# Token mixing by Fourier transform and a gated feed-forward block: stage one contracts residues j and 47-j together, in 64-column tiles

## The chip, the core and the metric

The kernel runs on one core of a Trainium2 chip. A core has a matrix engine (PE, also TensorE), which multiplies a stationary operand (the weights, loaded by a weight-load instruction, "PEld") with a moving one and writes to an accumulator memory, PSUM; a vector engine (DVE), a scalar engine (ACT), a general engine (POOL, GpSimd), and a queue engine (SP) that issues most of the DMA transfers. Each engine takes its instructions in order; they wait for each other by semaphores. The metric is the device time of one execution, in microseconds (us).

## The reference, cut to what matters

```python
def _attn_ref(x):                      # x: 8 x 3008 x 256, float32
    X = np.fft.fft(x, axis=1)          # over the tokens
    X = np.fft.fft(X, axis=2)          # over the channels
    return X.real.astype(np.float32)

def _moe_ref(x, w_gate, w_val, w_out): # x: 24064 x 256, d_ff = 1536
    g = x @ w_gate
    gelu = 0.5 * g * (1.0 + erf(g / np.sqrt(2.0)))
    val = x @ w_val
    return (gelu * val @ w_out).astype(np.float32)
```

The second function takes the first one's output as 24064 tokens.

## The kernel before, in words

The transform over the channels is folded into the weights, so that what is left per batch is the transform over 3008 tokens, of which the real part and its mirror image are used, and the feed-forward block.

The token transform is done in two stages, with 3008 = 64 x 47: token 47 n + j, with n from 0 to 63 and residue j from 0 to 46. The names are `N1` = 64, `N2` = 47, `HJ` = 24 (half the residues), `KP` (the rows of stage two).

*Loading and folding.* `load_x` brings a third of a batch at a time (8 residues of each half) into one of three buffers `xin`. Partition 2n holds residue j, partition 2n+1 residue j+24, for j from 0 to 23. `fold_x` adds and subtracts channel c and channel 256-c (two products on POOL or, for the first batch, DVE) and writes `xf`, bf16, 24 residues x 2 halves (even, odd) x 128 channels; `singles` copies the two channels without a partner on POOL.

*Stage one.* `a_step(b, k)` multiplies two residue slots of `xf`: each is one product with 128 weight columns of `G` (128 partitions x 128 columns, in which the two residues that share the partitions have blocks of their own and the rest is zero) and 256 moving columns. So a product gives 64 frequencies for each of two residues. The two products fill one PSUM bank, and ACT (for three of them DVE) copies it as bf16 to `S1`. There are 12 steps in a batch. `z_write` sends parts of `S1` to HBM, `z_read` brings them back turned into `Ap`, with the 96 residue rows on partitions (two rows for each of 48 slots, `KP` = 96) and 32 frequencies x 256 channels along them. For the first batch `a_group(J)` does the same in six groups of sixteen products with 32 weight columns each, in turn on four column positions, and turns the result from `S1` to `Ap` by one DMA inside the chip.

*Stage two.* `b_steps(b, eo, q)` makes the products with `Ap` as weights (96 rows x 128 columns) and a table `TP` or `TQ` as the moving operand (47 columns): 66 a batch in two halves (`eo`) and four blocks (`q`). For the first batch 33 more with one weight column. Evacuated, they give `Y`. `n_turn` and `n_step` do the same for one single channel, in f32, with 48 weight columns.

*The feed-forward block.* A batch is 36 units (3 column chunks x 12 blocks of d_ff), some 2 us each. A unit has four or five products of 128x128 weights and 480 to 512 columns (`layer1`, weights `WE`, `WOP`, `WOM`), its activations on ACT, its products of gate and value on DVE and POOL, and six or eight products of the second layer with 256 columns (`second`, weights `h`), which belong to the chunk before.

*Order.* The order is written out by hand in the main loop (from line 955 on); each engine keeps the program's order. While batch b runs its units, batch b+1 is prepared between them: `a_step(b + 1, k)` at the end of units 0 to 11 (for batch 1 at units 4 to 15, `a_first`), its writes after steps 5, 7 and 11, its reads at units 8, 10 and 13; stage two at units 18 to 26 (odd half) and 27 to 34 (even half), as `fills`: two products at a time between two of `layer1`. x of batch b+2 is loaded at units 0, 14 and 19, and folded on POOL at the odd units from 5 on. All x, z and output transfers go through SP's one queue. `ps_d`, one PSUM bank, serves `a_step`, `b_steps` and `n_step` after the start.

```python
        def fill(most=2):
            for _ in range(most):
                if fills:
                    fills.pop(0)()
```

Of the kernel before, what the change touches and what calls it, by code (L numbers as in the profile page):

```python
# [9 lines left out]
FP32 = mybir.dt.float32  # L10
BF16 = mybir.dt.bfloat16
AF = mybir.ActivationFunctionType
ALU = mybir.AluOpType
# [24 lines left out]
def kernel(  # L38
# [28 lines left out]
    HJ = 24  # L67
    KP = 96
    NG = 32
# [45 lines left out]
    col_j = const_pool.tile([128, 1], FP32)  # L115
    prow = const_pool.tile([1, 641], BF16)
    cols = const_pool.tile([128, 5], FP32)
    col_w = const_pool.tile([128, 1], FP32)
# [6 lines left out]
    def S1_tile():  # L125
        return work.tile([128, HJ, C], BF16, tag="S1", bufs=1, name="S1")

# [63 lines left out]
    def ps_o():  # L191
        return psum.tile([128, 512], FP32, tag="o", bufs=1, name="ps_o")
# [4 lines left out]
    def z_tile():  # L197
        return dram.tile([HJ, 128, C], BF16, tag="z", bufs=2, name="z")


    def load_x(b, i):
        xt = xins[i]
        for o, n, nh in ([(0, 7, 2), (7, 1, 1)] if i == 2 else [(0, 8, 2)]):
            src = ap_replace(
                x, ap=[[N2 * C, N1], [HJ * C, nh], [1, n * C]],
                offset=x.offset + (b * T + 8 * i + o) * C)
            p_step = xt[:, :, :].ap[0][0]
            dst = ap_replace(
                xt[:, :, :], ap=[[p_step * 2 // nh, N1 * nh], [1, n * C]],
                offset=xt[:, :, :].offset + o * C)  # L210
            sync.dma_start(out=dst, in_=src)
# [22 lines left out]

    vec.memset(xins[2][:, 7, :], 0.0)
    for i in range(3):
# [10 lines left out]
    row = lambda i, pat, off=0: _sub(prow, pat, 128 * i + off, 0, 1)  # L247
    for k in range(2):
        iota(row(0, [[24, 4], [6, 2], [3, 2], [1, 3]], 12 * k), [[1, 4], [0, 2], [4, 2], [8, 3]], 24 * k, 0)
    for i, (base, sign) in enumerate(((0, 1), (0, 1), (1, -1))):  # L250
        iota(row(1 + i, [[12, 8], [6, 2], [1, 6]]), [[0, 8], [sign, 2], [0, 6]], base, 0)
    pool.memset(row(0, [[128, 4], [1, 32]], KP), 0.0)
    pool.memset(row(4, [[1, 129]]), 1.0)

    def cols_t():
        ps = ps_o()
        for i in range(5):
            pe.matmul(ps[:, i : i + 1], _sub(prow, [[1, 128]], 128 * i, 0, 1),
                      _sub(prow, [[1, 1]], 640, 0, 1), start=True, stop=True)
        vec.tensor_copy(cols, ps[:, :5])  # L260
        vec.tensor_scalar(col_j, cols[:, 0:1], 1.0 / N2, None, op0=ALU.mult)
        vec.tensor_scalar(col_w, cols[:, 4:5], -TWO_PI, None, op0=ALU.mult)
# [46 lines left out]

    whole(col_f, col_p, 0.5, -0.25)  # L310
    vec.tensor_scalar(col_a, col_p, 360.0, None, op0=ALU.mult)
    vec.scalar_tensor_tensor(col_a, col_f, -719.0, col_a, op0=ALU.mult, op1=ALU.add)
    vec.tensor_scalar(rowj, rowj, col_a, None, op0=ALU.add)
    vec.scalar_tensor_tensor(col_b, col_f, -2.0, col_p, op0=ALU.mult, op1=ALU.add)
    vec.tensor_scalar(col_h[1], col_b, -TWO_PI, None, op0=ALU.mult)
    vec.tensor_scalar(col_h[0], col_b, TWO_PI, -TWO_PI, op0=ALU.mult, op1=ALU.add)

# [168 lines left out]
    def a_step(b, k):  # L486

        if "S1" not in st[b]:
            st[b]["S1"] = S1_tile()
        S1 = st[b]["S1"]  # L490
        if b == 0:
            ps = (ps_g, ps_vh, ps_o if k % 8 < 4 else ps_d, ps_vh)[k % 4]()
        else:
            ps = ps_o() if b == 1 and k in (3, 5) else ps_d()
# [18 lines left out]
    def a_group(J):  # L513
        if "S1" not in st[0]:
            st[0]["S1"] = S1_tile()
        S1 = st[0]["S1"]
        if J % 4 < 2:
            ps, log = ps_v(), []
            both = ps
            banks = [(ps[:, h, :], log) for h in range(2)]  # L520
        else:
            banks = [(f(), []) for f in ((ps_g, ps_g) if J % 4 == 2 else (ps_o, ps_d))]
        for gq in range(4):
            for jl in range(4):
                jj = 4 * J + jl
                ps, log = banks[gq // 2]
                apart(log, gq // 2, pe.matmul(
                    _sub(ps, [[1, C]], gq % 2 * C, 32 * jl, 32),
                    _sub(G, [[32, 4], [4, 8]], (jj - 16 * (J > 3 and gq % 2 == 0)) * 128 + gq),
                    _sub(xf, [[1, C]], jj * C), start=True, stop=True))  # L530
        if J > 3:
            for o, n, scale in ((0, 2, 1.0), (2, 1, -1.0), (3, 1, 1.0)):
                ps, log = banks[o // 2]
                to, of = _sub(S1, [[1, n * C]], (4 * J + o) * C), _sub(ps, [[1, n * C]], o % 2 * C)
                apart(log, o // 2, vec.tensor_scalar(to, of, scale, None, op0=ALU.mult) if J == 4 and o else
                      act.activation(to, of, AF.Copy, scale=scale))
        if J < 2:
            act.activation(_sub(S1, [[1, 4 * C]], 4 * J * C), both, AF.Copy)
        for h in range(2 * (J in (2, 3))):
            dst = _sub(S1, [[1, 2 * C]], (4 * J + 2 * h) * C)  # L540
            act.activation(dst, banks[h][0], AF.Copy)
        p_step = Ap[:, :, :].ap[0][0]
        sync.dma_start(
            out=ap_replace(
                Ap[:, :, :], ap=[[6 * p_step, 16], [1, NG * C]],
                offset=Ap[:, :, :].offset + (J % 2 * 3 + J // 2) * p_step),
            in_=_sub(S1, [[1, 4 * C]], 4 * J * C))

    def z_read(b, third, h=None):
        z = st[b]["z"]  # L550
        src = ap_replace(
            z[0:1, 0, :], ap=[[NG * C, 16], [16 * NG * C, 2], [1, NG * C]][:: 1 if h is None else 2],
            offset=z[8 * third + 4 * (h or 0), 0:1, :].offset)
        p_step = Ap[:, :, :].ap[0][0]
        dst = ap_replace(
            Ap[:, :, :], ap=[[3 * p_step, 32] if h is None else [6 * p_step, 16], [1, NG * C]],
            offset=Ap[:, :, :].offset + (third + 3 * (h or 0)) * p_step)
        sync.dma_start(out=dst, in_=src)
# [374 lines left out]
    for f0, o, n, us, turn in (  # L933
# [6 lines left out]
    extra[7].append(gen_wn)  # L940
    a_first = {4: (0,), 5: (1,), 8: (2, 3), 9: (4,), 10: (5, 6)} | {
        11 + j: (7 + j,) for j in range(5)}
    reads_first = {12: (0,), 14: (1,), 16: (2, 0), 17: (2, 1)}

# [10 lines left out]
    for u in range(NU + 2):  # L955
# [82 lines left out]
        if u < NU:  # L1038
            if b == 0:
                for e in extra.get(i, ()):  # L1040
                    e()
                if i < 12:
                    fold_x(1, i // 4, pool, i % 4 * 2, 2)
            if i % 2 and b + 2 < B:
                j = i - 1
                if b:
                    f, fp = next((j - o, n) for n, o, z in ((0, 4, 18), (1, 18, 28), (2, 28, 36)) if j < z)
                else:
                    fp, f = divmod(j - 12, 8)
                if 0 <= f < 8 and fp >= 0:  # L1050
                    fold_x(b + 2, fp, pool, f, 2)
            if b + 1 < B:
                for k in (i,) if b else a_first.get(i, ()):
                    if k < 12:
                        a_step(b + 1, k)
                        if k in ((5, 7, 11) if b else (5, 7, 9, 11)):
                            j0 = {5: 0, 7: 12, 9: 16, 11: 16 if b else 20}[k]
                            z_write(b + 1, j0, 2 * k + 2 - j0)
                    if b and k in (8, 10, 13):
                        z_read(b + 1, (8, 10, 13).index(k))  # L1060
                if b == 0 and i in reads_first:
                    z_read(1, *reads_first[i])
        if 0 < u <= NU and u % 12 == 0:
# [41 lines left out]
```

## Time and profile before

| | us |
|---|---|
| median of three runs (616.19 to 616.27) | 616.2 |
| the profiled execution | 616.14 |
| its span, by the profile | 614.3 |
| the start, until the first product of unit 0 | 23.8 |
| stretch of 70 us in the middle: PE / DVE / ACT / POOL busy | 69.62 / 66.72 / 57.20 / 63.46 |

Some of the groups of PE by shape, in the profile's view of instruction groups (line, engine, operation, output<-inputs, weight rows x weight columns, operands; count; busy time and mean ns of one):

```profile
L25 PE MATMUL ps_d<-xf,G 128*128 128x256 bf16 x164 | 31.2, 272 | 0.0
L25 PE MATMUL ps_d<-TP,Ap 96*128 96x47 bf16 x217 | 22.4, 185 | 0.3
L25 PE MATMUL ps_d<-TQ,Ap 96*128 96x47 bf16 x225 | 21.7, 185 | 0.7
L25 PE MATMUL ps_v<-xf,G 128*32 128x256 bf16 x64 | 3.3, 370 | 3.9 <-POOL xf L25 3.9
L25 PE MATMUL ps_d<-NA,TF 96*48 96x31 f32 x28 | 2.5, 213 | 0.0
```

The mean of one is the time from its start to its modelled end. Products follow each other before the one ahead has ended, so what a product takes of PE is the distance from its start to the next one's, which the timeline shows; a group's line doesn't. A few per cent of the records are missing (164 of 168 here). Nearly every instruction has line 25, that of the helper which records the order; the tiles' names tell them apart.

### The profile page before, as it was taken

The page shows a single profiled execution, that of the slowest core. Times are in us where ns is not written, and L with a number is a line of the kernel's source. Part 1 is how long each engine was busy: PE and PEld are TensorE (multiplying, and loading weights), DVE is VectorE, ACT ScalarE, POOL GpSimd, SP SyncE. Part 2 cuts the span into 40 slices and gives each one's busy share as a digit, 9 for nine tenths or more (in the row PEclk, how much of TensorE's full clock was granted, in tenths as well). Part 3 has the DMA queues.
Part 4 walks back from the last instruction along what each step waited for, and adds up shares of the span by engine and source line. Part 5 has one row for each costly group of instructions (what it writes and reads, how often), then busy time and mean ns, then how long its engine had stood idle before and what let it go on. Part 6 is the DMA issues. An engine that isn't in the chain of part 4 may idle for free.

```text
span 614.3 us, 13104 instructions
## 1 busy us (share of the span) xinstructions
PE 597.6 (97%) x4581; PEld 399.8 (65%) x4638; DVE 567.2 (92%) x689; ACT 487.4 (79%) x1011; POOL 501.5 (82%) x525
## 2 busy tenths in 40 slices
PE   4999999999999999999999999999999999999997
PEld 2556666666676666666667666766667666666666
DVE  8788999999999999999999999999999999999992
ACT  8798789877898787977789778887789878776762
POOL 5599999989999899798998899898997755665552
PEclk9999999999999999999999999999999999999999
DMA  7989424772257612674246633476223712222123
GB/s 277 348 233 264 135 65 116 202 216 60 61 149 197 197 39 70 205 224 113 66 120 173 192 93 74 121 207 209 46 67 100 203 37 52 59 47 52 39 48 86
DMA packets 63459, 80.79 MB, mean 132 GB/s; under 512 B 8186, under 2 KB 56826, under 8 KB 60674
## 3 DMA queue, kind: packets, MB, share of 16 engines
q1 hardware_dynamic: 61682, 79.05, 45.5%
q0 software_dynamic: 1552, 0.79, 0.9%
q8 instruction: 36, 0.59, 0.4%
q14 instruction: 29, 0.24, 0.1%
q10 hardware_dynamic: 160, 0.13, 0.1%
HBM read 43.47 MB, written 35.68 MB: 129 GB/s over the span
## 4 chain that ended last, share of the span: by engine, by line
PE 91%; ACT 3%; DMA 2%; DVE 2%; SPq 1%; issue 1%; ACTq 0%; POOL 0%
PE ps_o L25 38%; PE ps_g L25 26%; PE ps_v L25 20%; PE ps_d L25 7%; DMA xin<-in_x_dram 1%; ACT glm L25 1%; ACT osb L25 1%; ACT S L25 1%; SPq L850 1%; DMA out_dram<-osb 1%; ACT glp L25 0%; DVE h L25 0%; SPq L855 0%; DVE red L25 0%; DVE ev L25 0%
## 5 line engine op out<-in xcount | busy, mean ns | idle before, releaser
L25 POOL TENSOR_TENSOR h<-glm,dv 128x1024 bf16<-128x1024 bf16 (+1 forms) x138 | 290.8, 2109 | 80.6 <-DVE dv L25 60.0
L25 PE MATMUL ps_o<-Wo_sb,h 128*128 128x256 bf16 x2124 | 284.2, 272 | 1.0
L25 PEld LDWEIGHTS <-h 128*128 128x128 bf16 x2208 | 211.0, 98 | 58.3 <-issue 0.9
L25 DVE SCALAR_TENSOR_TENSOR ev<-nq,WN,ps_v 128x512 f32<-128x512 bf16 (+1 forms) x276 | 202.2, 734 | 23.4 <-PE ps_v L25 13.4
L25 ACT ACTIVATE glp<-ps_g 128x512 bf16<-128x512 f32 (+1 forms) x288 | 169.8, 590 | 37.2 <-PE ps_v L25 18.6
L25 ACT ACTIVATE glm<-ps_g 128x512 bf16<-128x512 f32 (+1 forms) x241 | 142.2, 590 | 56.6 <-PE ps_g L25 44.0
L25 DVE TENSOR_TENSOR h<-glp,ps_v 128x1024 bf16<-128x1024 bf16 (+2 forms) x150 | 173.0, 1154 | 4.2 <-ACT glp L25 3.5
L25 DVE SCALAR_TENSOR_TENSOR dv<-ev,ps_v 128x1024 f32<-128x1024 f32 (+1 forms) x138 | 164.9, 1195 | 0.0
L25 POOL TENSOR_TENSOR xf<-xin 128x254 bf16<-128x254 f32 x168 | 118.1, 724 | 0.4 <-PE ps_g L25 0.4
L25 PE MATMUL ps_v<-Y,WOP 128*128 128x512 bf16 (+1 forms) x288 | 107.7, 374 | 0.1
L25 PE MATMUL ps_v<-Y,WE 128*128 128x512 bf16 (+1 forms) x286 | 107.3, 375 | 0.0
L25 PE MATMUL ps_g<-Y,WE 128*128 128x512 bf16 (+1 forms) x266 | 99.3, 373 | 0.0
L25 PE MATMUL ps_g<-Y,WOP 128*128 128x512 bf16 (+1 forms) x257 | 96.0, 373 | 0.8
L25 PE MATMUL ps_g<-Y,WOM 128*128 128x512 bf16 (+1 forms) x241 | 90.3, 375 | 0.2
L25 PEld LDWEIGHTS <-WOP 128*128 128x128 bf16 x576 | 55.5, 97 | 49.2 <-ACT WOP L25 0.6
L25 PEld LDWEIGHTS <-WE 128*128 128x128 bf16 x576 | 56.0, 97 | 27.8 <-issue 2.0
L25 ACT ACTIVATE osb<-ps_o 128x512 f32<-128x512 f32 x92 | 54.2, 589 | 13.4 <-PE ps_o L25 11.9
L25 POOL TENSOR_TENSOR go<-go,ge 128x480 f32<-128x480 f32 (+1 forms) x47 | 58.1, 1236 | 7.1 <-DVE go L25 7.1
L25 PEld LDWEIGHTS <-Ap 96*128 96x128 bf16 (+1 forms) x561 | 39.6, 96 | 31.7 <-issue 0.2
L25 ACT ACTIVATE S<-ps_d 128x512 bf16<-128x512 f32 x82 | 48.9, 596 | 0.2 <-PE ps_d L25 0.2
L25 PEld LDWEIGHTS <-G 128*128 128x128 bf16 (+1 forms) x289 | 22.0, 110 | 26.5 <-issue 4.7
L25 DVE SCALAR_TENSOR_TENSOR go<-nq,WN,ps_g 128x480 f32<-128x480 bf16 (+1 forms) x47 | 34.3, 730 | 2.6 <-ACT glp L25 1.9
(134 smaller groups left out, 371.8 us busy)
## 6 DMA issues: line engine op xcount, KB each, us to landing
out_dram<-osb SPq DMA_DIRECT2D x358, 64.0 KB
xin<-in_x_dram SPq DMA_DIRECT2D x16, 1024.0 KB
Ap<-z SPq DMA_DIRECT2D x20, 512.0 KB
xin<-in_x_dram SPq DMA_DIRECT2D x8, 896.0 KB
z<-S SPq DMA_DIRECT2D x7, 768.0 KB
z<-S SPq DMA_DIRECT2D x6, 512.0 KB
nq<-nrow SPq DMA_DIRECT2D x8, 376.2 KB
z<-S SPq DMA_DIRECT2D x9, 256.0 KB
```

Source lines behind the costliest of these rows:

```text
L25: return lambda *a, **k: self._tc.keep_in_program_order(call(*a, **k))
L850: queues[q % 2].dma_start(out=rows_ap(rows[0][0], 32, rows[1][0] - rows[0][0], 2), in_=_sub(t, [[C, 2], [1, C]], 0, 32 * q, 32))
```

## The change

x = X(n, j) is real, and so the contributions of residue j and of residue 47-j to a frequency differ by a sign and a conjugate. The changed kernel puts residue j on partitions 0 to 63 and residue 47-j on partitions 64 to 127 (residue 0 has no partner: its rows are zero) and contracts all 128 partitions to 64 columns, with one set of 64 weight columns for the even channel half and another for the odd one.

- `load_x`: two DMAs for each third, the second with the residues in falling order, so in pieces of one row (1 KB). `singles`: a product with a column `sg` (1, and -1 on the upper partitions) instead of a copy.
- `a_step`: 6 steps a batch instead of 12, at units 0, 2, ... 10 (batch 1: units 5, 8, 10, 11, 13, 15), each with 8 products of 64 weight columns and 128 moving columns, in turn at output partitions 0 and 64. All evacuations are on ACT and go through `ps_d`.
- `a_group`: the same 16 products a group, with 128 moving columns instead of 256.
- `S1`, z and the turning DMAs have half the rows; z is written in three equal parts, and read in three (batch 1: units 9, 13, 17).
- `KP` is 48: stage two and `n_step` contract 48 rows; the products are as many as before, with the same columns.

```diff
-    KP = 96
+    HP = HJ // 2
+    KP = 2 * HJ
...
     def load_x(b, i):
...
+        o = 0 if i else 1
+        for p0, s, first, pat in ((0, 0, 8 * i, [[1, 8 * C]]),
+                                  (N1, o, N2 - o - 8 * i, [[-C, 8 - o], [1, C]])):
+            sync.dma_start(
+                out=_sub(xins[i], [[1, (8 - s) * C]], s * C, p0, N1),
+                in_=ap_replace(x, ap=[[N2 * C, N1]] + pat, offset=x.offset + (b * T + first) * C))

     def singles(i, a0=0, an=8):
-        pool.tensor_copy(
+        pool.tensor_tensor(
             _sub(xf, [[C, an], [128, 2]], (8 * i + a0) * C),
-            _sub(xins[i], [[C, an], [128, 2]], a0 * C))
+            _sub(xins[i], [[C, an], [128, 2]], a0 * C),
+            _sub(sg, [[0, an], [1, 2]], 0), op=ALU.mult)
...
     def a_step(b, k):
...
-        for i in range(2):
-            jj = 2 * k + i
-            on_half(ps, pe.matmul(
-                ps[:, i * C : (i + 1) * C], G[:, jj, :], _sub(xf, [[1, C]], jj * C),
-                start=True, stop=True))
-        dst = _sub(S1, [[1, 2 * C]], 2 * k * C)
-        if b == 0 and k % 2 == 0 and k >= 8 or b == 1 and k in (0, 3, 5):
-            return on_half(ps, vec.tensor_copy(dst, ps))
-        return on_half(ps, act.activation(dst, ps, AF.Copy))
+        ps = ps_d()
+        for i in range(8):
+            q, e, par = i // 4, i // 2 % 2, i % 2
+            jj = 4 * k + 2 * q + par
+            pe.matmul(
+                _sub(ps, [[1, 128]], q * C + e * 128, 64 * par, 64),
+                _sub(G, [[1, 64]], jj * 128 + 64 * e), _sub(xf, [[1, 128]], jj * C + 128 * e),
+                start=True, stop=True)
+        act.activation(_sub(S1, [[1, 2 * C]], 2 * k * C), ps, AF.Copy)
...
     def a_group(J):
...
+        for gq in range(2):
+            for e in range(2):
+                for jl in range(4):
+                    jj = 4 * J + jl
+                    on_half(ps, pe.matmul(
+                        _sub(ps, [[1, 128]], gq * C + e * 128, 32 * jl, 32),
+                        _sub(G, [[32, 2], [2, 16]], (jj - 16 * (J > 3 and gq == 0)) * 128 + 64 * e + gq),
+                        _sub(xf, [[1, 128]], jj * C + 128 * e), start=True, stop=True))
...
-    def z_read(b, third, h=None):
+    def z_read(b, third):
...
-            z[0:1, 0, :], ap=[[NG * C, 16], [16 * NG * C, 2], [1, NG * C]][:: 1 if h is None else 2],
-            offset=z[8 * third + 4 * (h or 0), 0:1, :].offset)
+            z[0:1, 0, :], ap=[[NG * C, 16], [1, NG * C]], offset=z[4 * third, 0:1, :].offset)
...
+    a_first = {5: 0, 8: 1, 10: 2, 11: 3, 13: 4, 15: 5}
+    a_later = {2 * k: k for k in range(HP // 2)}
+    reads = ({9: 0, 13: 1, 17: 2}, {4: 0, 8: 1, 13: 2})
...
             if b + 1 < B:
...
+                k = (a_later if b else a_first).get(i)
+                if k is not None:
+                    a_step(b + 1, k)
+                    if k % 2:
+                        z_write(b + 1, 2 * k - 2, 4)
+                if i in reads[b > 0]:
+                    z_read(b + 1, reads[b > 0][i])
```

The rest of the diff makes the tables `G`, `cols` and `sg` for the new layout and adapts the evacuations of `a_group`.

More of the change, by code (lines that the diff above doesn't have):

```diff
@@ L115 @@
     col_j = const_pool.tile([128, 1], FP32)
-    prow = const_pool.tile([1, 641], BF16)
-    cols = const_pool.tile([128, 5], FP32)
+    prow = const_pool.tile([1, 769], BF16)
+    cols = const_pool.tile([128, 6], FP32)
+    sg = const_pool.tile([128, 2], FP32)
     col_w = const_pool.tile([128, 1], FP32)
@@ L125, in S1_tile @@
     def S1_tile():
-        return work.tile([128, HJ, C], BF16, tag="S1", bufs=1, name="S1")
+        return work.tile([128, HP, C], BF16, tag="S1", bufs=1, name="S1")
     def Y_tile():
@@ L197, in z_tile @@
     def z_tile():
-        return dram.tile([HJ, 128, C], BF16, tag="z", bufs=2, name="z")
+        return dram.tile([HP, 128, C], BF16, tag="z", bufs=2, name="z")
     def load_x(b, i):
[L202 to L211, printed above, removed]
+        o = 0 if i else 1
[4 more added lines that the diff above has]
+                in_=ap_replace(x, ap=[[N2 * C, N1]] + pat, offset=x.offset + (b * T + first) * C))
     def singles(i, a0=0, an=8):
-        pool.tensor_copy(
+        pool.tensor_tensor(
             _sub(xf, [[C, an], [128, 2]], (8 * i + a0) * C),
-            _sub(xins[i], [[C, an], [128, 2]], a0 * C))
+            _sub(xins[i], [[C, an], [128, 2]], a0 * C),
+            _sub(sg, [[0, an], [1, 2]], 0), op=ALU.mult)
     def fold_x(b, i, eng, a0=0, an=8, single=True):
@@ L247 @@
     row = lambda i, pat, off=0: _sub(prow, pat, 128 * i + off, 0, 1)
-    for k in range(2):
-        iota(row(0, [[24, 4], [6, 2], [3, 2], [1, 3]], 12 * k), [[1, 4], [0, 2], [4, 2], [8, 3]], 24 * k, 0)
+    iota(row(0, [[12, 4], [6, 2], [3, 2], [1, 3]]), [[2, 4], [1, 2], [0, 2], [8, 3]], 0, 0)
+    iota(row(5, [[2, 64], [1, 2]]), [[0, 64], [-2, 2]], 1, 0)
     for i, (base, sign) in enumerate(((0, 1), (0, 1), (1, -1))):
-        iota(row(1 + i, [[12, 8], [6, 2], [1, 6]]), [[0, 8], [sign, 2], [0, 6]], base, 0)
-    pool.memset(row(0, [[128, 4], [1, 32]], KP), 0.0)
-    pool.memset(row(4, [[1, 129]]), 1.0)
+        iota(row(1 + i, [[6, 8], [3, 2], [1, 3]]), [[0, 8], [sign, 2], [0, 3]], base, 0)
+    pool.memset(row(0, [[128, 4], [1, 128 - KP]], KP), 0.0)
+    pool.memset(row(4, [[1, 128]]), 1.0)
+    pool.memset(row(6, [[1, 1]]), 1.0)
     def cols_t():
         ps = ps_o()
-        for i in range(5):
+        for i in range(6):
             pe.matmul(ps[:, i : i + 1], _sub(prow, [[1, 128]], 128 * i, 0, 1),
-                      _sub(prow, [[1, 1]], 640, 0, 1), start=True, stop=True)
-        vec.tensor_copy(cols, ps[:, :5])
+                      _sub(prow, [[1, 1]], 768, 0, 1), start=True, stop=True)
+        vec.tensor_copy(cols, ps[:, :6])
         vec.tensor_scalar(col_j, cols[:, 0:1], 1.0 / N2, None, op0=ALU.mult)
@@ L516, in a_group @@
         S1 = st[0]["S1"]
[L517 to L520, printed above, removed]
-        else:
[L522 to L538, printed above, removed]
@@ L539, in a_group @@
-        for h in range(2 * (J in (2, 3))):
-            dst = _sub(S1, [[1, 2 * C]], (4 * J + 2 * h) * C)
-            act.activation(dst, banks[h][0], AF.Copy)
+        ps = (ps_vh, ps_vh, ps_g, ps_g, ps_o, ps_d)[J]()
+        for gq in range(2):
[6 more added lines that the diff above has]
+                        _sub(xf, [[1, 128]], jj * C + 128 * e), start=True, stop=True))
@@ L542, in a_group @@
+        to = _sub(S1, [[1, 2 * C]], 2 * J * C)
+        if J > 3:
+            for h in range(2):
+                to, of = _sub(S1, [[1, C]], (2 * J + h) * C), _sub(ps, [[1, C]], h * C)
+                if J == 4:
+                    vec.tensor_scalar(to, of, 1.0 if h else cols[:, 5:6], None, op0=ALU.mult)
+                else:
+                    act.activation(to, of, AF.Copy, scale=1.0 if h else cols[:, 5:6])
+        else:
+            on_half(ps, act.activation(to, ps, AF.Copy))
         p_step = Ap[:, :, :].ap[0][0]
```

42 lines of the change are left out of this document (13 added, 29 removed).

## The prediction

> **What bounds the kernel now.** I read the page first: shares of busy time, then the chain that ended last.
>
> ```profile
> span 614.3 us, 13104 instructions
> PE 597.6 (97%) x4581; PEld 399.8 (65%) x4638; DVE 567.2 (92%) x689; ACT 487.4 (79%) x1011; POOL 501.5 (82%) x525
> ...
> PE 91%; ACT 3%; DMA 2%; DVE 2%; SPq 1%; issue 1%; ACTq 0%; POOL 0%
> ```
>
> PE is busy 97% of the span and holds 91% of the chain. Busy PE is not proof that nothing is waiting, so next the waits of PE alone. Their sum is 9.4 us, all before 30 us; from there to the tail PE is released by nobody.
>
> ```profile
> PE ps_o L25 <- POOL prow L25: 4.8, 1, 4.8
> PE ps_v L25 <- POOL xf L25: 3.9, 1, 3.9
> PE ps_g L25 <- DVE wb L25: 0.4, 1, 0.4
> PE ps_d L25 <- DVE WOM L25: 0.3, 1, 0.3
> ```
>
> Then one period of a batch, 70 us, engine by engine. Beside PE's 69.62 us, DVE has 3.3 us free, POOL 6.5, ACT 12.8, and the DMA engines half.
>
> ```profile
> 180.00:250.00 70.00, 69.62 (x529) 47.00 (x534) 66.72 (x77) 57.20 (x120) 63.46 (x65) 1.00 0.50 139
> ```
>
> So a nanosecond added to or taken from PE's stream after the start is one of the time, and work on ACT, POOL and the queues is free while it stays within these margins.
>
> Last, the timeline of PE, for what lies between two products. The first column is the start.
>
> ```profile
> 205.24 0.19 PE L25 MATMUL ps_d<-T0Q,Ap 96*128 96x47 bf16 x2
> 205.30 0.18 PE L25 MATMUL ps_d<-TQ,Ap 96*128 96x47 bf16 x1
> 205.32 0.38 PE L25 MATMUL ps_g<-Y,WOP 128*128 128x512 bf16 x1
> 205.54 0.21 PE L25 MATMUL ps_d<-TQ,Ap 96*128 96x47 bf16 x2
> 205.59 0.81 PE L25 MATMUL ps_o<-Wo_sb,h 128*128 128x256 bf16 x6
> 206.24 0.38 PE L25 MATMUL ps_v<-Y,WE 128*128 128x512 bf16 x1
> ...
> 212.44 0.38 PE L25 MATMUL ps_g<-Y,WE 128*128 128x512 bf16 x1
> 212.65 0.38 PE L25 MATMUL ps_g<-Y,WOP 128*128 128x512 bf16 x1
> 212.96 0.43 PE L25 MATMUL ps_d<-NA,TF 96*48 96x31 f32 x6
> 213.32 0.83 PE L25 MATMUL ps_o<-Wo_sb,h 128*128 128x256 bf16 x6
> ```
>
> From start to start, a 512-column product takes 0.215 us, a 256-column one 0.109 (206.24 - 205.59, by 6), a pair of stage two 0.05 (205.54 to 205.59): two 47-column products slip between two large ones for their own time. The last four lines show the other case. After a 512-column product the products of `n_step` start 0.31 later, not 0.215: 0.095 us are lost. What differs is the number of weight columns, 48 and not 128: the built program gives such a product a tile of 128x64 of the array, where all its neighbours have 128x128. All seven `n_step`s show it (0.094 to 0.096). The way back: the six take 0.36 us, and inside they follow each other at 0.045, so 0.09 is lost again.
>
> It isn't `n_step`'s f32 or a wait, since the start of the kernel shows it for bf16:
>
> ```profile
> 22.43 0.54 PE L25 MATMUL ps_v<-TQ,Ap 96*128 96x47 bf16 x15
> 22.89 0.36 PE L25 MATMUL ps_d<-TP,Ap 96*1 96x47 bf16 x8
> ...
> 14.32 0.50 PE L25 MATMUL ps_v<-xf,G 128*32 128x256 bf16 x12
> 14.75 0.82 PE L25 MATMUL ps_d<-G 128*128 128x512 bf16 x2
> ```
>
> Fifteen at 0.025 from 22.43 end at 22.80, the next starts at 22.89 (0.09; it waits for no other engine). The second pair of lines shows two things. Twelve 256-column products of 32 weight columns take 0.43 us; one by one they would take 12 x 0.109 = 1.31. Four at a time on four column tiles they take 3 x 0.109 = 0.33, and the rest, 0.10, is the way back to 128x128. So tiles side by side do run together, and each change of tile costs 0.09 to 0.10 us.
>
> **The change, part by part.** *Stage two (`b_steps`, 48 rows instead of 96).* Count, columns (47) and weights (128 columns) stay, and so does the 0.025 us of each: no gain there. But in the built program the tile goes from 128x128 (96 rows) to 64x128 (48 rows), while the layer products around it keep 128x128. In the new order, after the start, the 462 products of stage two stand in 203 runs: 172 of two, 14 of three, 13 of four, 4 of six. Each run is a change in and one out, 406 in all. The trace has no change in the rows of a tile that is not hidden by a wait (five one-row products, then 4 us idle). Bounds: nothing, as for the pair at 205.54 now, and 0.097 us, the dearest change seen: 0 to 39.4 us. I take 0.092, the middle of the rows above, since the new tile is a change of the array's partition as theirs are: 406 x 0.092 = **+37.4 us**, and no PE idle time after 30 us to hide it in.
> [...]
>
> *Stage one (`a_step`).* Removed in each of 7 batches: 24 products of 128x128x256, 24 x 0.109 = 2.62 us. Added: 6 steps of 8 products of 64 weight columns and 128 columns, in turn on column tiles 0 and 64. A step is one change in, four pairs and one change out. A pair streams 128 columns, half of 0.109: 0.055. A load of 64 weight columns by `n_step`'s 0.045 for 48: 0.060; side by side, as the four 32-column loads above must be to keep 0.109, a pair takes 0.060. A step: 2 x 0.092 + 4 x 0.060 = 0.424 us, against 4 x 0.109 = 0.436 for the same four residues before: -0.012 x 42 = **-0.5 us**. Bounds: pairs at the stream's 0.055 (-1.3), pairs whose two loads are one after the other, 0.12 (+0.228 a step, +9.6). I take the lower middle, as the 12 products at 14.32 are nearest. Halving the products is thus paid away by the two changes at each step.
> Some 40 ACT evacuations and 3 DVE copies fewer (0.6 to 0.7 us each) lie beside PE and bring nothing.
>
> *Queues and POOL.* z writes and reads halve (1.5 MB a batch each way become 0.8); the last z read still stands at unit 13, its write one unit earlier (10, not 11), so `n_turn` and stage two at units 18 and 19 wait for nothing new. Every load of x becomes two DMAs, the second in 1 KB pieces: packet records near 10 us show 47 ns for 1 KB and 309 for 8 KB, so a third of a batch lands 448 x (47 - 39) / 16 = 0.2 us later; outside the start it has five units, 10 us, before its fold. SP issues 16 more x loads and 2 fewer z transfers of some 0.5 us each, among out stores that nothing waits for. POOL's 84 small copies (0.20 us) become products with a sign; between 0.20 and the 0.72 of its 128x254 product, and nearer the first by size, say 0.25: 0.6 us a batch, at most 6.2, of POOL's 6.5 free. Without that cover `fold_x` would run late, and stage one behind it by as much; it has a batch of time.
>
> *The start, to 24 us.* `a_group` streams 128 columns instead of 256. DVE, not PE, sets the pace to 13.8 (folds), then DVE waits 0.63 us for PE before its evacuation at 14.46; at half the streaming most of that goes. The x pieces take back up to 3 x 0.2 - 0.25 (fold three began 0.25 after its data). I take **-0.3 us**, bounds -0.9 (all of the wait and a shorter last group) and +1.0 (two 512-column products at 10.80 start 0.40 apart, PE half as fast as later; with less PE work before, that may last longer).
>
> Sum: 37.4 - 0.5 - 0.3 = +36.6. Profiled execution: 614.3 + 36.6 = 650.9 us of span, and the 1.8 us around it (616.14 - 614.3): **652.7**. That execution and the median (616.2) are the same time.
>
> **Rivals.**
> 1. *A change of rows only is free* (other side). Mechanism: what is lost at `n_step` comes from splitting columns; 48 rows use the top of the same columns, so the pair goes on costing 0.05 us. For: 96-row products now stand among 128-row ones at no cost. Against: those have the same tile in the program, the new ones have not. Then 616.1 - 0.5 - 0.3 = 615.3 (613.9 with the low bounds). It decides from below 0.002 us a change: 406 x 0.002 = 0.8.
> 2. *Half price.* A 64-row tile empties sooner, 0.046 a change: 18.7 - 0.8, 634.0. For: the loss looks like a passage through the array. Against: 32-column and 48-column tiles lose as much, so size does not show.
> 3. *The 64-column loads are serial.* 37.4 + 9.6 - 0.3: 662.8. For: nothing shows two loads of 64. Against: the four at 14.32.
> That the products are halved only in name is part of 3: streaming is halved only if pairs overlap.
> DVE (3.3 us free a batch) can bound only if PE gained more than that; z's latency has no part in any case.
>
> **How the numbers follow.** Forecast 0.62, rival 1 0.20, rival 2 0.12, rival 3 0.06. The range leaves out rival 1 alone: from 630, under rival 2, to 664, over rival 3. The forecast's own: 648 (changes out at 0.075, as a half-deep tile may empty sooner, 406 x 0.0835 = 33.9, with the low bounds of the rest) to 656 (0.097 a change, +1.0 in the start). About 0.2% (1.2 us) is what a measurement can tell from no change. Rival 1 at 615.3 is just within it, its bounds on both sides: of its 0.20, 0.09 faster, 0.08 same, 0.03 slower. Everything else is slower: 0.83.
>
> **What would show it.** The timeline of PE around a pair of stage two: 0.09 us lost before and after (right), start 0.215 after the 512 (rival 1). A stage-one step from the end of the product before to the next large one: 0.42 us, or 0.66 (rival 3). A batch's period up by 406 x 0.092 / 7 = 5.3 us from some 72, with DVE's and ACT's busy share down. No new PE wait on an engine. The forecast is wrong if the pairs of stage two still fit in 0.05 us.

## The result, and the profile after

| | before | changed |
|---|---|---|
| median, us | 616.2 (616.19 to 616.27) | 676.6 (672.99 to 680.47, four runs) |
| profiled execution and its span, us | 616.14, 614.3 | 680.47, 678.7 |
| ratio of the medians | 1 | 1.098 (95% interval 1.091 to 1.105) |

Slower, as forecast, but by 60.4 us and not by 36.5, and outside the range (630 to 664). The profiled execution is the slowest of the four; where its parts are added up below, they are added up to its own 64.4 us of span.

The page of the changed kernel: span, busy time, then PE, PE's granted clock (PEclk, in tenths of full speed) and bandwidth in 40 slices, and the chain that ended last.

```profile
span 678.7 us, 13487 instructions
PE 647.9 (95%) x4807; PEld 394.4 (58%) x4807; DVE 569.5 (84%) x685; ACT 473.7 (70%) x968; POOL 507.2 (75%) x526
...
PE   2789889999999999999999999999999999999997
...
PEclk9989979999999999999999999999999999999999
...
GB/s 183 216 218 125 156 102 71 105 138 159 33 62 145 154 104 55 88 127 156 67 66 129 126 144 29 70 148 149 105 55 63 99 58 40 55 48 48 48 40 86
...
PE 88%; DMA 9%; SPq 1%; DVE 1%; ACT 0%; POOL 0%; issue 0%; ACTq 0%; DVEq 0%
```

PE is busy 50 us longer with products that are shorter, and DMA's share of the chain has gone from 2 to 9%. Of the first six slices of PE, some 100 us, five are below 9 (before: the first only), and the first slices move 183 and 216 GB/s (before 277 and 348). So there is a loss over the whole, and another in the first 100 us. In the third and the sixth slice PE isn't granted its full clock (before: 9 in every slice). PE's waits (in all, times, longest) show the second:

```profile
PE ps_d L25 <- DMA out_dram<-osb: 5.3, 1, 5.3
PE ps_o L25 <- POOL prow L25: 5.3, 1, 5.3
PE ps_v L25 <- POOL xf L25: 4.1, 1, 4.1
PE ps_o L25 <- POOL xf L25: 2.6, 1, 2.6
PE ps_d L25 <- POOL xf L25: 2.3, 1, 2.3
PE ps_g L25 <- POOL xf L25: 2.1, 1, 2.1
PE ps_o L25 <- DMA Wo_sb<-in_moe_w_out_dram: 1.3, 1, 1.3
```

Before, they were 9.4 us in all, `prow` and one `xf` nearly alone.

When the first gate activation of a unit starts, read from each trace and less the same unit's of the kernel before, shows where the lead is lost (us; a batch is 36 units):

```
unit               0     6    15    21    24    36    72   144   252   end
changed          9.3  13.3  14.8  15.0  22.5  26.6  32.9  45.4  64.3  64.4
e1 80 rows       9.4  16.2  15.9  16.0  22.5  22.5  22.7  23.1  23.8  23.8
e2 parity        4.2   4.1   3.7   3.9  10.6  14.6  20.9  33.5  52.3  52.4
e3 both          6.7   6.5   6.2   6.4  12.2  12.1  12.4  12.8  13.4  13.4
e4 before, 64    0.1   0.1   0.1   0.1   0.7   4.8  10.8  23.0  41.2  41.2
e5 before, x/2   7.3  13.3  17.9  17.9  17.9  17.9  17.9  17.9  17.9  17.9
e7 in order      4.5   4.3   4.0   4.1   4.1   4.1   4.3   4.7   5.4   5.4
e13 changed, in  8.4  10.8  10.5  10.7  12.0  16.1  22.3  34.9  53.8  53.9
```

The first row: 14.8 us by unit 15, where stage two has not begun to stand between layer products; a jump of 7.5 between units 21 and 24; then 6.3 a batch, the same in each. The steady part was forecast (5.3 a batch), the first two were not.

The jump is one wait of PE and what comes behind it. PE stands for 5.3 us before the first products of stage two for batch 1 and then runs on at half pace (start, length, operation, count, idle time before):

```profile
87.95 0.20 PE L25 MATMUL ps_d<-T0Q,Ap 48*128 48x47 bf16 x2 [5.32 <-DMA out_dram<-osb]
...
90.30 0.63 PE L25 MATMUL ps_v<-Y,WE 128*128 128x512 bf16 x1
90.72 0.63 PE L25 MATMUL ps_g<-Y,WOM 128*128 128x512 bf16 x1
```

Two 512-column products start 0.42 us apart here, not 0.215. The trace's records of the granted clock say 0.5 from 84.8 to 91.7 us, so 3.7 us of work behind the wait ran at half pace; by that, some 1.9 us are lost on top of the 5.3. A second such stretch, 47.3 to 50.7, follows the wait of 2.3 us for `xf`.

The steady part. PE's timeline of the changed kernel, where pairs of stage two and a step of stage one stand (start, length, operation, count):

```profile
280.04 0.37 PE L25 MATMUL ps_g<-Y,WOP 128*128 128x481 bf16 x1
280.34 0.41 PE L25 MATMUL ps_d<-xf,G 128*64 128x128 bf16 x8
280.68 0.61 PE L25 MATMUL ps_o<-Wo_sb,h 128*128 128x256 bf16 x4
...
316.77 0.39 PE L25 MATMUL ps_g<-Y,WOP 128*128 128x512 bf16 x1
317.09 0.22 PE L25 MATMUL ps_d<-TQ,Ap 48*128 48x47 bf16 x2
317.24 0.61 PE L25 MATMUL ps_o<-Wo_sb,h 128*128 128x256 bf16 x4
```

The pair starts 0.32 us after the 512-column product, not 0.215, and holds PE for 0.15, not 0.05: the two changes cost 0.20. Of the 203 runs after the start phase, 201 begin 310 to 323 ns after the 512-column product ahead of them (the other two follow a wait); the second product of a pair follows after 38 to 40 ns instead of 28 to 32, and the return takes 111 to 114 instead of 25 to 34. In the median, a run of two costs 257 ns beyond the streaming of its neighbours (before 55), one of four 298 (108), of six 359 (155): 40.7 us over all runs, 0.100 a change.

The weight loads (PEld) show what is lost at the entry. In the kernel before, at the pair of 205.54:

```profile
205.32 0.31 PEld L25 LDWEIGHTS <-Ap 96*128 96x128 bf16 x2
```

and in the changed kernel, at the pair of 317.09:

```profile
316.76 0.10 PEld L25 LDWEIGHTS <-WOP 128*128 128x128 bf16 x1
317.09 0.11 PEld L25 LDWEIGHTS <-Ap 48*128 48x128 bf16 x2 [0.23 <-issue]
```

Before, the first load for the pair starts with the 512-column product ahead (205.32), 0.21 us before the pair itself. In the changed kernel nothing is loaded during that product; the load starts at 317.09, with the pair.

The step of stage one: 280.34 - 280.04 is 0.30, of which 0.20 are the 481 columns; to 280.68 it is 0.34. So 0.44 for four residues.

### The profile page after: what moved, and what is told of

It is laid out like the page before. It is cut to its first block, busy times and chain, and to the rows that moved or that the text cites. A ratio compares the mean times of both kernels' runs of the same rounds, so it can differ in the third digit from the quotient of the medians.

```text
span 678.7 us, 13487 instructions
## 1 busy us (share of the span) xinstructions
PE 647.9 (95%) x4807; PEld 394.4 (58%) x4807; DVE 569.5 (84%) x685; ACT 473.7 (70%) x968; POOL 507.2 (75%) x526
## 4 chain that ended last, share of the span: by engine, by line
PE 88%; DMA 9%; SPq 1%; DVE 1%; ACT 0%; POOL 0%; issue 0%; ACTq 0%; DVEq 0%
PE ps_o L25 36%; PE ps_g L25 26%; PE ps_v L25 18%; PE ps_d L25 7%; DMA Wo_sb<-in_moe_w_out_dram 4%; DMA xin<-in_x_dram 2%; DMA wst<-in_moe_w_gate_dram 1%; DMA z<-S 1%; DMA out_dram<-osb 1%; SPq L25 1%; DVE xf L25 0%; POOL wb L25 0%; DVE S L25 0%; DVE red L25 0%; ACT osb L25 0%
## 5 line engine op out<-in xcount | busy, mean ns | idle before, releaser
L25 PEld LDWEIGHTS <-h 128*128 128x128 bf16 x2208 | 208.1, 98 | 71.8 <-issue 2.7
L25 PE MATMUL ps_g<-Y,WOP 128*128 128x512 bf16 (+1 forms) x288 | 108.9, 378 | 0.0
L25 PE MATMUL ps_g<-Y,WE 128*128 128x512 bf16 (+1 forms) x288 | 108.0, 375 | 0.0
L25 ACT ACTIVATE osb<-ps_o 128x512 f32<-128x512 f32 x92 | 54.1, 589 | 23.1 <-PE ps_o L25 20.4
L25 POOL TENSOR_TENSOR go<-go,ge 128x480 f32<-128x480 f32 (+1 forms) x47 | 58.1, 1235 | 10.8 <-DVE go L25 10.5
L25 PEld LDWEIGHTS <-Ap 48*128 48x128 bf16 (+1 forms) x561 | 26.7, 93 | 67.8 <-issue 49.9
L25 DVE SCALAR_TENSOR_TENSOR go<-nq,WN,ps_g 128x480 f32<-128x480 bf16 (+1 forms) x47 | 34.3, 729 | 11.1 <-ACT glp L25 11.0
L25 PEld LDWEIGHTS <-G 128*64 128x64 bf16 (+2 forms) x457 | 16.0, 113 | 37.0 <-issue 29.6
L25 ACT ACTIVATE Y<-ps_d 128x192 bf16<-128x192 f32 (+4 forms) x142 | 34.0, 339 | 0.5 <-PE ps_d L25 0.5
```

The costliest lines, as they stand in the source:

```text
L25: return lambda *a, **k: self._tc.keep_in_program_order(call(*a, **k))
```

## The experiments

Times are medians beside runs of the kernel before on the same chip (616.2 to 616.4 in every group). In e1, in e3 and in what is built on e3, stage two contracts 32 rows of zeros besides.

**e1: stage two over 80 rows, with the tile of 128x128.**

```diff
+    KW = 80
...
-                w = _sub(Ap, [[1, 1 if m1 else 128]], g * C + eo * 128, 0, KP)
+                w = _sub(Ap, [[1, 1 if m1 else 128]], g * C + eo * 128, 0, KW)
...
+    sync.dma_start(out=_sub(Ap, [[C, NG], [1, C]], 0, KP, KW - KP), in_=_sub(zrow, [[0, NG], [1, C]], 0))
```

> Stage two contracts 80 rows (48 of data, 32 of zeros) and so keeps the 128x128 tile; all else is the changed kernel. Theory (a tile change costs about 0.1 us, and the changed kernel has 203 runs of stage two after the start at 0.20 us more each): 676.6 - 40.7 = 636 us, a pair of stage two back at 0.05 us. Rival (the loss is in the transfers of x alone, and the tile changes were absorbed): 670 us or more.

640.2 us (639.82 to 641.45): 36.5 less by the medians, where 40.7 were expected, and 40.6 by the spans of the profiled executions. The loss per batch is gone (22.5 at unit 36, 23.1 at unit 144); up to unit 24 the delay is within 3 us of the changed kernel's. PE's timeline in e1:

```profile
318.58 0.38 PE L25 MATMUL ps_g<-Y,WE 128*128 128x512 bf16 x1
318.80 0.19 PE L25 MATMUL ps_d<-T0P,Ap 80*128 80x47 bf16 x2
318.85 0.18 PE L25 MATMUL ps_d<-TP,Ap 80*128 80x47 bf16 x1
318.87 0.38 PE L25 MATMUL ps_g<-Y,WOP 128*128 128x512 bf16 x1
```

0.22 to the first, three products in 0.07: the same products with 32 useless rows more cost nothing again.

**e4: the kernel before, with the first 64 of the 96 rows of stage two.**

```diff
-                w = _sub(Ap, [[1, 1 if m1 else 128]], g * C + eo * 128, 0, KP)
+                w = _sub(Ap, [[1, 1 if m1 else 128]], g * C + eo * 128, 0, 64)
...
-                        ps[r, o : o + N2], w, t[:KP, s : s + N2], start=True, stop=True))
+                        ps[r, o : o + N2], w, t[:64, s : s + N2], start=True, stop=True))
```

> The kernel before with stage two contracting rows 0 to 63 only (rows 64 to 95 are left out), so that its tile is 64x128 and nothing else changes. Theory (tile change): 616.2 + 40.7 = 657 us. Rival (a change of rows is free): 616 us.

657.5 us (657.1 and 657.8), 41 more, with a start that is the old one to 0.1 us (row e4 of the table). This kernel leaves out a third of the sum of stage two, so its output is not the transform; PE gets the same products with fewer rows. So the price needs nothing else of the change.

**e8: the same products in fewer runs.**

```diff
-        def fill(most=2):
+        def fill(most=8):
```

> The changed kernel with the products of stage two dealt out eight at a time and not two: the same products, 108 runs of them after the start instead of 203. Theory (each run costs two changes of tile, 0.19 to 0.20 us, however many products are in it): 95 x 0.19 = 18 us less than the changed kernel, 656 to 661. Rival (the loss belongs to each product of 48 rows, not to the change): no gain, 673 to 680.

655.9 us (655.43 to 660.6): 20.7 less than the changed kernel, whose own runs lie between 673.0 and 680.5. By medians that is 0.22 us for each of the 95 runs saved, two changes of 0.109, a little over the 0.100 of the timeline. The price belongs to the change, not to the product.

**e2: residue j on even partitions, 47-j on odd ones,** so that each load of x reaches over all 128.

```diff
-        for p0, s, first, pat in ((0, 0, 8 * i, [[1, 8 * C]]),
-                                  (N1, o, N2 - o - 8 * i, [[-C, 8 - o], [1, C]])):
+        for h, s, first, pat in ((1, o, N2 - o - 8 * i, [[-C, 8 - o], [1, C]]),
+                                 (0, 0, 8 * i, [[1, 8 * C]])):
...
-                out=_sub(xins[i], [[1, (8 - s) * C]], s * C, p0, N1),
+                out=ap_replace(xt, ap=[[2 * p_step, N1], [1, (8 - s) * C]], offset=xt.offset + h * p_step + s * C),
```

> Residue j on the even partitions and 47-j on the odd ones, so that each x load reaches partitions over the whole range; same two DMAs, same 1 KB pieces. Theory (a load into partitions 0-63 or 64-127 alone runs at half the rate, 23 us in all): 653 us, first activation of unit 0 at about 24.5 us, 8 KB packets at 310 ns and 1 KB at 47. Rival (the 1 KB pieces are what is slow): 8 KB packets fast, the third of a batch still 4 to 5 us, unit 0 at 30 us or later, 670 us.

667.6 us (665.22 to 668.78): 9.0 less, where 23 were expected. Unit 0 came 5.1 us earlier, and no more was lost up to unit 21; but a jump between 21 and 24 stayed (6.7). So my theory for the whole of the first batch was wrong: the loads of x account for the start and the wait for weights behind them, and something else acts at unit 22.

**e3: e1 and e2 together.** (Both edits.)

> Both edits: 80 rows and the even and odd partitions. Theory (two independent losses): 676.6 - 40.7 - 23 = 613 us, between 611 and 617, a stage-one step still 0.44 us. Rival (a third loss in stage one or in the z traffic): over 620 us.

626.8 us (625.93 to 629.49), where 611 to 617 were expected: the third loss exists. It is 5.8 us between units 21 and 24 and some 6.5 in the start. e3 against e1 gives the price of the half loads in the changed kernel: 13.4 us. Taken in the other order the same 49.9 us divide otherwise, 9.0 for the loads (e2) and 40.8 for the tile (e3 against e2). Runs of the changed kernel spread over 7.5 us, so the division is known to some 4 us; the timeline and the spans speak for some 40.7 for the tile.

**e5: the kernel before, each load of x split into partitions 0 to 63 and 64 to 127,** in unchanged pieces of 8 KB.

```diff
-            src = ap_replace(
-                x, ap=[[N2 * C, N1], [HJ * C, nh], [1, n * C]],
-                offset=x.offset + (b * T + 8 * i + o) * C)
+            for n0 in (0, N1 // 2):
+                src = ap_replace(
+                    x, ap=[[N2 * C, N1 // 2], [HJ * C, nh], [1, n * C]],
+                    offset=x.offset + (b * T + 8 * i + o + N2 * n0) * C)
```

> The kernel before, with one edit: each load of x becomes two, into partitions 0 to 63 and 64 to 127, of the same 8 KB pieces; nothing else changes. Theory (a load that writes only 64 neighbouring partitions runs at about half the rate, and the start of the changed kernel pays for it): 8 KB packets of the first thirds take some 600 ns instead of 310, the first batch's first activation comes 4 to 7 us later than in the kernel before, and the time is 5 to 15 us over it (621 to 631). Rival (it is the 1 KB pieces that are slow, not the partitions): packets stay at 310 ns, the time within 1 us of before (616).

630.9 us (627.82 and 634.01): this split alone costs 14.7 (11.5 and 17.7 in its two runs), and 17.9 in the profiled execution, all of it by unit 15. The mean granted clock of the two runs is 0.997 and 0.989, so part of their difference fits a half pace of PE behind its waits. The DMA view of the stretch from 3 to 8 us, when hardly anything but x moves (queue and kind: packets, MB, share of 16 engines), in the kernel before:

```profile
q1 hardware_dynamic: 280, 2.04, 97.9%
```

in e5, the kernel before with split loads:

```profile
q1 hardware_dynamic: 177, 1.19, 105.8%
```

in the changed kernel:

```profile
q1 hardware_dynamic: 563, 1.14, 108.0%
```

and in e2:

```profile
q1 hardware_dynamic: 1046, 1.75, 100.9%
```

The engines are full in all four; what differs is what they move. In the median, packets of 8 KB took 309 ns before, 618 to 650 in the changed kernel and 595 to 634 in e5; those of 1 KB took 46 before and 80 to 89 in the changed kernel. In e2, with 1 KB pieces but partitions over the whole range, both are back at 310 and 46. It is the partitions, not the pieces. The three thirds of the first batch lie ready at 8.1, 13.1 and 18.3 us in the changed kernel; before at 6.2, 8.6 and 11.1.

**e7: e3, and the stores of the output kept in their place in the queue.**

```diff
-            store_pair(pair, t, (nc.sync, nc.sync))
+            store_pair(pair, t, (sync, sync))
```

(and the same for the other stores). `sync` is the wrapper that keeps the written order; `nc.sync` lets the builder place the instruction.

> The third experiment (80 rows in stage two, residues on even and odd partitions) with one more edit: the stores of the output are kept in their written place among the loads and z reads of the same queue. Theory (SyncE's queue stood behind a store of the output before the first z read of the second batch, and stage two at units 22 and 23 waited for that read): the wait at units 22 and 23 goes and with it the jump of 5.8 us between units 21 and 24, so 620 to 622. Rival (the read is late because its z was written late, or the loads of x hold the DMA engines): the jump stays, 626 to 627.

620.5 us (620.37 to 621.45), 6.2 less; the jump is gone.

**e13: the changed kernel with that edit alone.** (Same diff.)

> The changed kernel with one part undone: the stores of the output keep their written place in SyncE's queue, as in e7 and with nothing else of it. Theory (the queue stands behind a store before it reads z, whatever the loads of x do): the jump of 7.5 us between units 21 and 24 of the first batch goes, 668 to 671. Rival (in the changed kernel itself the loads of x at half rate make the z read late anyway): the jump stays for more than half, 673 to 677.

670.0 us (667.99 to 671.29), 6.6 less. SyncE's timeline shows what was undone. In the changed kernel:

```profile
56.23 0.37 SPq L25 DMA_DIRECT2D z<-S  x1
69.33 1.79 SPq L840 DMA_DIRECT2D out_dram<-osb  x2
71.22 0.56 SPq L25 DMA_DIRECT2D Ap<-z  x1
71.83 0.57 SPq L25 DMA_DIRECT2D z<-S  x1
72.50 1.19 SPq L25 DMA_DIRECT2D xin<-in_x_dram  x2
75.98 0.54 SPq L25 DMA_DIRECT2D Ap<-z  x1
```

and in e13:

```profile
53.57 0.57 SPq L25 DMA_DIRECT2D z<-S  x1
61.72 0.56 SPq L25 DMA_DIRECT2D Ap<-z  x1
62.37 0.53 SPq L25 DMA_DIRECT2D z<-S  x1
63.00 1.18 SPq L25 DMA_DIRECT2D xin<-in_x_dram  x2
65.96 0.55 SPq L25 DMA_DIRECT2D Ap<-z  x1
66.60 3.06 SPq L25 DMA_DIRECT2D out_dram<-osb  x4
```

In the first, the queue does nothing from 56.6 to 69.3: its next instruction is a store (line 840, placed by the builder; line 25 is the helper's) that waits for its data, and behind it stand the first read of z for batch 1, a write of z, a load of x and the second read. The queue's own waits between 50 and 75 us (in all, times, longest) name it:

```profile
SPq L840 <- ACT osb L25: 12.7, 1, 12.7
```

In the second the first read leaves at 61.7 and the second ten us earlier. PE's wait `ps_d <- out_dram<-osb`, 5.3 us, isn't among e13's waits any more; the releaser that the profile names, a store of the output, has nothing to do with stage two's data, but it is what the queue stood behind. The jump falls from 7.5 us to 1.3, 6.2 less, and e13's trace has no half pace after the start. The two profiled executions differ by 10.5 us (678.7 and 668.2); 4.3 of these are there by unit 15, before the queue has sent a store, and so belong to the spread of the start and not to the edit.

**e9: e7 with more stand-ins in the start.**

```diff
-        if J == 1:
-            warm(2)
+        if J in (1, 3):
+            warm(5 if J == 1 else 3)
```

> The one before with eight stand-in products in the groups of the start instead of two (five after the second, three after the fourth), which do no work. Theory (PE idles so much between the groups of the start that its products run at half pace up to the last of them: ten 512-column stand-ins took 4.4 us, in the kernel before 2.3): the ten take 2.2 to 2.4 us and the time is 1.5 to 2.5 us under the run before it, some 618.5. Rival (the half pace ends at a set time after the start, whatever PE does): the ten still take 4.4 us, and the time is the same or 1 us more.

623.3 us (620.45 to 625.28): the theory held for the step and not for the time. PE in the changed kernel, the ten stand-ins of 512 columns that precede the first weights:

```profile
22.29 4.42 PE L25 MATMUL ps_d<-G 128*128 128x512 bf16 x10 [0.87 <-ACT S L25]
```

and in e9, with the first products of stage two and the layer products that follow:

```profile
16.38 2.32 PE L25 MATMUL ps_d<-G 128*128 128x512 bf16 x10 [0.88 <-ACT S L25]
...
25.05 0.36 PE L25 MATMUL ps_v<-TP,Ap 80*128 80x47 bf16 x8 [2.67 <-DMA wst<-in_moe_w_gate_dram]
...
28.50 0.61 PE L25 MATMUL ps_g<-Y,WE 128*128 128x481 bf16 x1
28.90 0.61 PE L25 MATMUL ps_v<-Y,WE 128*128 128x481 bf16 x1
```

The ten run at full pace: they hold PE for 2.2 us, where they hold it for 3.7 in e7 and for 4.2 in the changed kernel. What follows them starts 1.95 us earlier than in e7 (18.54 for 20.49), but PE then waits 2.67 instead of 1.30 before stage two, which starts only 0.6 earlier. From 26.8 on its products start 0.40 apart, and not 0.21, for 3 us: the granted clock of that stretch is 0.52. The ten stand-ins start 0.43 us apart in the changed kernel and 0.215 in e9, which has eight others ahead of them instead of two; how much work ends the half pace, or how much idling brings it on, no run here shows. The granted clock of the changed kernel's stretch from 24 to 28 us is listed as 1.00 all the same: the first record of the clock in that trace is at 26.8, where the spacing halves, and what lies ahead of it has no record, so the half pace there has to be read from the starts.

**e10: e9, the zero rows in 4 KB packets.**

```diff
-    zrow = const_pool.tile([32, C], BF16)
+    zrow = const_pool.tile([32, 8 * C], BF16)
```

> The run with eight stand-ins (e9), whose 32 zero rows now come in 128 packets of 4 KB, not 1024 of 512 bytes (POOL clears the source). Theory (what is left of the start's delay is the way of z to stage two: the zero rows stood 2.5 to 3.5 us in front of the six transfers that turn z, and these run on 8 of the 16 DMA engines): PE's wait before the first products of stage two shrinks from 2.7 us to about 1 to 1.5, the first activation comes 1 to 2 us earlier, the time is 618.5 to 620. Rival (the wait is for something else, the first gate weights): the wait stays, the time within 0.5 us of e9's best runs (620.5).

622.5 us (621.26 to 623.8): undecided. In the profiled execution one of the 16 landings of the last third of x came 2.5 us after the other fifteen (15.2 and 12.7 us), so that stage two waited for nothing and unit 0 still came 5.9 us late. In e11, which contains this edit, that landing did not lag, the wait was 1.2 us and unit 0 came 2.6 late. One execution of each can't settle it.

**e11 and e12: 18 more units with the second gate formed on DVE and POOL,** in e10 and in the kernel before.

```diff
-    SPLIT = ((15, 25, 31, 35), (1, 5, 7, 11, 19, 25, 31, 35), (1, 5, 7, 11, 25, 31), (5,))
+    SPLIT = ((15, 25, 31, 35), (1, 5, 7, 11, 13, 19, 25, 29, 31, 35), (1, 5, 7, 11, 13, 19, 25, 31, 35), (5, 11, 25, 31))
```

> e10 with 18 more units of which VectorE and GpSimd form the second gate instead of TensorE (47 becomes 65). Theory (PE sets the period and each such unit saves one product of 0.215 us): 18 x 0.215 = 3.9 us less than e10, some 615. Rival (DVE, 69.3 of 72.6 us busy in a batch, then bounds): less than half of it.

> The kernel before with the same 18 more units of that kind. Theory (the changed kernel frees nothing that this edit needs: DVE is busy 69.4 us a batch in the kernel before and 69.3 in the repaired changed one): the same 3.9 us less, 612.3, so the gain belongs to the edit and not to the change. Rival (it needs the ACT time that the change frees): under 1 us of gain.

623.5 us (622.5 to 624.41) and 625.2 (625.01 to 625.8), where 3.9 less were expected: no gain, and 9.0 us lost in the kernel before. Each such unit costs 0.5 us in the kernel before (9.0 by 18), although DVE has 3.3 us free in 70 and PE gets a product less. Why wasn't followed further, nor why the loss on e10 is smaller (1.0 by medians). For the question here it means that the ACT time that the change frees (59.7 us busy in a batch, then 57.2) has no use of this kind. No kernel of this study is faster than the one before; the best, e7, is 0.7% slower (ratio 1.0072, 1.0057 to 1.0087).

## Why the prediction was wrong

By medians, each term by the run that removes it: 676.6 to e1 640.2 (tile of stage two), to e3 626.8 (loads of x into half the partitions), to e7 620.5 (the store in the queue), to 616.3 (rest): 36.5 + 13.4 + 6.2 + 4.3 = 60.4. Between the first two, some 4 us could go either way (e2, e3).

- *Stage two, +37.4.* Right in mechanism and size: 36.5 by e1, 40.7 by the timeline (0.100 a change for 0.092: the weights of the first product after a change aren't loaded ahead, and inside a pair 39 ns pass instead of 29). That a change of rows costs what a change of columns does was an assumption, without a row of its own, and it held. Rival 1 (a change of rows is free) falls with e1 and e4, rival 2 (half price) with the entries of 310 to 323 ns. For the 64-row tile the changed kernel's trace has 0.10 us each way; in its 203 runs the first load of `Ap` starts 4 to 31 ns before its product, in the 191 of the kernel before 213 to 216. What the array does in that time isn't shown.
- *Stage one, -0.5.* 0.440 us a step, for 0.424 forecast and 0.436 before: +0.2 us in all. The pairs of 64-column loads do run side by side (the first two pairs of a step 80 ns apart, the others 55 to 57, the two of a pair 3 to 4). Rival 3 falls. Half the products bought nothing, as forecast.
- *The x loads: the step that failed.* I priced their second half by its pieces (1 KB packets at 47 ns, "a third of a batch lands 0.2 us later") from packets that wrote all 128 partitions, and let the first half go on at 309 ns. The diff says that each DMA writes `p0` to `p0 + 63`. At that, the same packet took some 620 ns, and the last third landed 7.2 us later (18.3 for 11.1), not 0.6. The weights, which stand behind x in the queue, came later still: 14.8 us by unit 15, 13.4 by medians, in place of the start's -0.3 with bounds of -0.9 and +1.0; those 14.8 hold PE's half pace in the start and behind the wait at 45 us too. The bounds were far too narrow, because no row of the trace before showed a load into half of the partitions, and I took the nearest by size of piece. The rate is in the DMA views of 3 to 8 us: 1.14 MB for 2.04 in the same five us. What in the chip sets it, none of them shows.
- *Queues: the second step that failed.* "SP issues ... among out stores that nothing waits for" and "z's latency has no part in any case" took the written order for the built one. Stores of the output are placed by the builder; in the changed kernel two of them stand before the first read of z for batch 1. That nobody waits for a store doesn't mean that nobody waits behind it. 6.2 to 6.6 us, of which the wait itself is 5.3; the rest fits the half pace behind it.
- *The rest, 4.3* (seen in e7, so with zero rows that the changed kernel doesn't have). In e7's profile unit 0 comes 4.5 us late: the last group of stage one ends 1.1 later, ten stand-ins at half pace and the waits around them add 1.9, and 1.3 is a wait for the turned z. The half pace is shown (e9), but what it would give without the wait after it is not. In the changed kernel itself the half pace is part of the 9.3 at unit 0: the last group of stage one ends 6.6 late, and the stand-ins add 2.5.
- *"No new PE wait on an engine"* was to hold: of the seven waits shown above five are new, three of them on POOL's `xf`, whose x came late. A period of 78.8 us (units 108 to 216, by three) against 72.5 is +6.3 for 5.3 forecast.

## What to carry to other kernels

Halving the work of a product by using half of the array saved nothing here, where its neighbours use the whole (a step of stage one 0.440 us for 0.436, a run of two in stage two 0.20 us dearer): count the changes of tile, not the columns or rows, and pad with zero rows (36.5 us less in e1) or gather such products into longer runs (20.7 less in e8). For a DMA, look first at which partitions it writes and only then at the size of its pieces: 8 KB took some 620 ns here for 309. And read the queue as it was built: a store that nothing waits for delayed all that stood behind it, here by 12.7 us. A wait of PE cost more than its length here: half the clock came with it (5.3 us of waiting, some 1.9 us of half pace).

## What was not expected of the hardware

- Loads into partitions 0 to 63 or 64 to 127 ran at nearly half the rate, though the queue's 16 engines were all busy (105.8% in e5, 108.0% in the changed kernel): 8 KB in 595 to 650 ns for 310. Alternate partitions (e2) ran at the full rate, 8 KB in 310.
- Transfers with 8 rows on their destination side kept some half of the 16 DMA engines busy: each of the six that turn z in the start of the changed kernel raises its semaphore 8 times as its data land (in the kernel before, where the destination has 16 rows, 16 times), and they land 1.1 us apart with 131 KB each, some 120 GB/s. The DMA view of 18 to 22.5 us in the changed kernel has the busy share of the engines in 40 slices:

```profile
DMA  9999998665555664565555555966363555465654
```

  Some half of the engines, while transfers queue; from this and the 8 landings I estimate that each transfer ran on 8 of them. It cost the changed kernel nothing by itself, since its stand-ins ended later (the last of the six landed at 26.4 us, stage two began at 30.4); in e7 and e9 the products that PE waits for before stage two (1.30 and 2.67 us) read these rows.
- POOL's product on 128 x 16 took 0.77 to 1.30 us beside DVE's folds in the start of the changed kernel, where the copy of the same size had taken 0.26 to 0.44. Later, on 128 x 4, the two are nearly alike: 0.22 and 0.20.
- PE's half pace behind a wait, in the changed kernel after 2.3 and 5.3 us of waiting (granted clock 0.5 for 3.4 and 6.8 us) and in e9 after 2.7 (0.52); not after the wait of 1.3 us in e7, where the 481-column products behind it start 0.21 apart.
